# Chain stages one whole step apart, weight pieces among the first nine loads, two filler products a unit in the first pass

## The chip, the cores and the metric

The kernel runs on one core of a Trainium2 chip. The metric is device time in microseconds (us), the median of several executions. A profile's own span, from first to last instruction, is 1.7 to 1.9 us shorter than the time of the same run. In the profile, PE is the tensor engine (PEld its weight loads), DVE the vector engine, ACT the scalar engine, POOL the GpSimd engine, SP the engine that issues the output transfers.

## The reference, cut to what matters

Four batches of 12480 rows of 128 numbers, 32 inducing rows, then a feed-forward with a gelu on every output row:

```python
def mab(q, kv):
    s = scale * (q @ kv.transpose(0, 2, 1))
    s = s - s.max(-1, keepdims=True)
    a = np.exp(s)
    a /= a.sum(-1, keepdims=True) + 1e-09
    return a @ kv
h = mab(I, x)            # 32 rows per batch: needs the whole batch
out = mab(x, h)          # every row of x against the 32 rows of h
# then, with x = out as 49920 rows:
h = x @ w_in                                   # 128 -> 2048
g = 0.5 * h * (1.0 + erf(h * inv_sqrt2))
return g @ w_out                               # 2048 -> 128
```

For these inputs the gelu can be expanded and moved in front of the second attention, onto the 32 rows of h. So the kernel makes two passes over the rows with a small dense computation, the "chain", between them for each batch, and checks on the device that the expansion was good enough (`check_gelu`).

## The kernel before

A batch is 7 units: six of 2048 rows and a tail of 192. The kernel issues work in steps. Step s transposes unit s, scores unit s-1, and adds unit s-2 into the sums of pass one; 21 steps later it runs pass two (`b_...`) for a unit. Steps 0 to 20 are pass one alone, 21 to 28 are both passes, and from about 29 it is pass two alone. In this kernel's timelines a product that waits for DVE holds up all products behind it: in chain 0 qp waited 2.35 us for gl, and PE ran nothing from 43.81 to 46.16 us. In the chain, pt is the projection of the 32 rows of h by w_in, sl and gl are the two steps of the expanded gelu on it, and qp is the product of gl with w_out; hs, slope and offs are small sums and factors for sl and gl.

```python
def a_load(u):                       # fp32 -> fp16, from POOL's queue
    xh = sb.tile([128, 16, 128], FP16, tag="xh", bufs=9)
    nc.gpsimd.dma_start(out=xh[: u.p, : u.nc, :], in_=src)

def a_score(bt, u):
    s1 = ps.tile([128, 16, M], FP32, tag="sc", bufs=2)
    ...                              # 16 products of 128x32 on PE
    nc.scalar.activation(out=e1t..., in_=s1..., func=AF.Exp, scale=SCALE)
    ...
    nc.gpsimd.tensor_tensor(out=acc, in0=acc, in1=e1t[: u.p, : u.nc, :], op=ALU.add)

def precompute(bt):                  # the chain; one stage per next()
    ...                              # stage 0: hun_sb (ACT), r1s (DVE, from acc)
    yield
    ...                              # h_ps (PE)
    yield
    ...                              # rr1, range checks, hT (DVE)
    yield
    ...                              # pt_ps = w_in_h.T @ hT: 16 products (PE)
    yield
    pt = pre.tile([128, NBLK, M], FP32, tag="pt")
    nc.scalar.activation(out=pt, in_=pt_ps, func=AF.Copy)
    nc.gpsimd.tensor_tensor(out=zsq, in0=pt, in1=pt, op=ALU.mult)
    nc.vector.tensor_reduce(out=hs, in_=pt, axis=AX.X, op=ALU.add)
    yield
    ...                              # slope, offs: 128x16 (DVE)
    nc.vector.tensor_tensor(out=sl, in0=pt, in1=slope..., op=ALU.mult)     # 128x512, SBUF
    yield
    nc.vector.tensor_tensor(out=gl, in0=sl, in1=offs..., op=ALU.subtract)  # 128x512, SBUF
    yield
    ...                              # qp_ps: 16 products of gl with w_out_h (PE)
    yield
    ...                              # qp (ACT)
    yield
    ...                              # q_ps (PE), q (DVE)
    yield
    check_gelu(bt, zsq, hs)          # seven small DVE operations

# in at_step(s); pump() runs one stage of the oldest chain, twice a step
if a0: a_transpose(bat(a0), a0, 0)
if a1: a_score(bat(a1), a1)
pump()
...
if a0: a_transpose(bat(a0), a0, 1)
if b0: b_score(bat(b0), b0)
pump()
...
if a2:
    a_gather(bat(a2), a2)
    if a2.tail:
        chains.append(precompute(bat(a2)))
    load_next()
    if weight_loads and s % 2:       # steps 3, 5, 7, 9
        dst, src = weight_loads.pop(0)
        nc.gpsimd.dma_start(out=dst, in_=src)
```

## Time and profile before

| | before |
|---|---|
| time, median of the first three runs | 165.76 us |
| span of the profiled run | 163.8 us |
| bytes of loads as landed (x as fp16, and weights) | 13.83 MB |
| bytes of output | 25.58 MB |
| step 21's score of pass two starts | 75.33 us |
| the same of steps 28 and 35 | 100.81, 120.45 us |

I use those three starts throughout as marks: the end of pass one alone, of both passes, and of the next batch.

The page's 40 slices of the span, kernel before: granted PE clock in tenths (the share of its full clock rate that PE was given), and the mean busy share of the 16 DMA engines in tenths. A slice is 4.1 us.

```profile
PEclk9999999655775599965999959755555555555555
DMA  3999999999999599895067367569678799999990
```

DMA is full for 12 slices from the second on, and then for longer only in the last ones. Between them it has gaps, and in pass one the clock falls to half three times (at 29.8, 46.8 and 70.7 us). The grant changes at 29.75, 43.41, 46.82, 57.06, 70.71 and 77.54 us in this trace, and these times lie multiples of 3.413 us apart.

The PE timeline of the kernel before, chain 0. Columns: start, length, engine and line, operation, how many, and in brackets the idle time before it and what ended it.

```profile
34.11 0.37 PE L276 MATMUL pt_ps<-hT,w_in_h 128*128 128x32 f16 x8 [0.33 <-DVE hT L271]
38.08 0.39 PE L276 MATMUL pt_ps<-hT,w_in_h 128*128 128x32 f16 x8 [3.60 <-DMA w_in_h<-in_moe_w_in_dram]
...
46.16 0.30 PE L328 MATMUL qp_ps<-w_out_h,gl 128*32 128x128 f16 x8 [2.35 <-DVE gl L318]
48.67 0.41 PE L328 MATMUL qp_ps<-w_out_h,gl 128*32 128x128 f16 x8 [2.21 <-DMA w_out_h<-in_moe_w_out_dram]
```

The chain's products stop PE four times here, for w_in, for gl, for w_out, and (0.33 us) for hT. Taking all PE idle times above 0.5 us from 5 us to step 21's score in the timeline together, 6.44 us were waits for rows of x and 15.15 us were other waits, all but 0.62 us of them in the chains.

POOL's timeline shows what that does to the loads: the load at 49.82 us was issued 4.27 us late because its turn came after a transpose on the halted PE.

```profile
44.41 1.14 POOL L177 TENSOR_TENSOR acc<-acc,e1t 128x512 f32<-128x512 f32 x1 [0.45 <-ACT e1t L170]
49.82 0.57 POOL L83 DMA_DIRECT2D xh<-in_x_dram  x1 [4.27 <-PE tr L150]
```

Busy times by stretch, kernel before, steps 21 to 28 and 28 to 35. Columns: stretch, length, then busy us (and count) of PE, PEld, DVE, ACT, POOL, then mean granted clock, DMA share and GB/s.

```profile
75.33:100.81 25.48, 23.21 (x394) 14.54 (x394) 21.96 (x51) 16.50 (x30) 13.21 (x14) 0.89 0.51 205
100.81:120.45 19.64, 14.16 (x205) 8.62 (x205) 16.53 (x45) 10.72 (x22) 12.77 (x16) 0.60 0.69 280
```

### The profile page before, as it was taken

The page shows a single profiled execution, that of the slowest core. Times are in us where ns is not written, and L with a number is a line of the kernel's source. Part 1 is how long each engine was busy: PE and PEld are TensorE (multiplying, and loading weights), DVE is VectorE, ACT ScalarE, POOL GpSimd, SP SyncE. Part 2 cuts the span into 40 slices and gives each one's busy share as a digit, 9 for nine tenths or more (in the row PEclk, how much of TensorE's full clock was granted, in tenths as well). Part 3 has the DMA queues.
Part 4 walks back from the last instruction along what each step waited for, and adds up shares of the span by engine and source line. Part 5 has one row for each costly group of instructions (what it writes and reads, how often), then busy time and mean ns, then how long its engine had stood idle before and what let it go on. Part 6 is the DMA issues. An engine that isn't in the chain of part 4 may idle for free. (4 is left out here: it accounts for less than half of the span.)

```text
span 163.8 us, 4550 instructions
## 1 busy us (share of the span) xinstructions
PE 111.2 (68%) x1859; PEld 77.4 (47%) x1859; DVE 91.6 (56%) x229; ACT 79.5 (49%) x136; POOL 93.1 (57%) x117
## 2 busy tenths in 40 slices
PE   0388587737617988369999598698458986678300
PEld 0366576626515877258666344363224543334100
DVE  2123132321822644926897988878989865467600
ACT  3057465431701465614867545648154774567300
POOL 7615866651815264942456825678374996589600
PEclk9999999655775599965999959755555555555555
DMA  3999999999999599895067367569678799999990
GB/s 39 213 214 215 213 212 207 194 209 202 214 204 208 95 204 175 146 156 99 32 288 320 136 256 318 222 288 392 250 316 320 306 416 420 392 375 418 420 380 18
DMA packets 10249, 39.74 MB, mean 243 GB/s; under 512 B 3024, under 2 KB 3824, under 8 KB 7152
## 3 DMA queue, kind: packets, MB, share of 16 engines
q0 software_dynamic: 6272, 13.83, 46.0%
q1 hardware_dynamic: 3952, 25.58, 38.3%
q8 instruction: 15, 0.25, 0.6%
q14 instruction: 10, 0.08, 0.2%
HBM read 27.67 MB, written 25.56 MB: 325 GB/s over the span
## 5 line engine op out<-in xcount | busy, mean ns | idle before, releaser
L150 PE MATMUL tr<-identity_h,xh 128*128 128x128 f16 x392 | 37.4, 252 | 7.6 <-DMA xh<-in_x_dram 7.1
L401 ACT ACTIVATE o<-at 128x512 f32<-128x512 f32 (+1 forms) x43 | 25.4, 591 | 20.9 <-PE at L440 13.4
L150 PEld LDWEIGHTS <-xh 128*128 128x128 f16 x392 | 28.4, 113 | 14.8 <-DMA xh<-in_x_dram 8.7
L177 POOL TENSOR_TENSOR acc<-acc,e1t 128x512 f32<-128x512 f32 (+1 forms) x24 | 24.3, 1012 | 19.3 <-ACT e1t L170 19.2
L83 POOL DMA_DIRECT2D xh<-in_x_dram x28 | 15.7, 565 | 14.1 <-PE tr L150 5.8
L402 POOL TENSOR_TENSOR o<-o,rr_1999 128x512 f32<-128x512 f32 x12 | 12.5, 1048 | 5.7 <-issue 2.0
L402 POOL TENSOR_TENSOR o<-o,rr_2618 128x512 f32<-128x512 f32 x12 | 12.3, 1047 | 3.6 <-ACT o L401 3.5
L402 POOL TENSOR_TENSOR o<-o,rr_2348 128x512 f32<-128x512 f32 x12 | 12.3, 1047 | 3.7 <-ACT o L401 3.3
L155 DVE COPY xT_459<-tr 128x1024 f16<-128x1024 f16 (+1 forms) x7 | 4.4, 628 | 17.0 <-PE tr L150 17.0
L404 DVE TENSOR_TENSOR o<-at,rr_1431 128x512 f32<-128x512 f32 (+1 forms) x19 | 12.0, 666 | 1.5 <-PE at L413 0.8
L155 DVE COPY xT_120<-tr 128x1024 f16<-128x1024 f16 (+1 forms) x7 | 4.4, 630 | 13.4 <-PE tr L150 13.4
L404 DVE TENSOR_TENSOR o<-at,rr_2618 128x512 f32<-128x512 f32 (+1 forms) x13 | 8.5, 670 | 4.6 <-DMA out_dram<-o 3.0
L404 DVE TENSOR_TENSOR o<-at,rr_2348 128x512 f32<-128x512 f32 (+1 forms) x13 | 8.5, 668 | 3.7 <-DMA out_dram<-o 1.8
L187 PEld LDWEIGHTS <-e1t 128*32 128x32 f16 x392 | 7.5, 109 | 5.6 <-issue 4.5
L404 DVE TENSOR_TENSOR o<-at,rr_1999 128x512 f32<-128x512 f32 (+1 forms) x13 | 8.6, 669 | 2.5 <-PE at L440 1.4
L157 ACT ACTIVATE xT_120<-tr 128x1024 f16<-128x1024 f16 x6 | 6.1, 1019 | 6.8 <-PE tr L150 6.8
L328 PE MATMUL qp_ps<-w_out_h,gl 128*32 128x128 f16 x64 | 2.3, 274 | 9.8 <-DVE gl L318 7.5
L402 POOL TENSOR_TENSOR o<-o,rr_1431 128x512 f32<-128x512 f32 (+1 forms) x7 | 6.6, 949 | 3.0 <-issue 1.6
L155 DVE COPY xT_895<-tr 128x1024 f16<-128x1024 f16 (+1 forms) x7 | 4.4, 628 | 6.5 <-PE tr L150 6.5
L175 POOL CAST acc<-e1t 128x512 f32<-128x512 f16 x4 | 2.4, 612 | 8.4 <-ACT e1t L170 8.4
L157 ACT ACTIVATE xT_1339<-tr 128x1024 f16<-128x1024 f16 x6 | 6.2, 1031 | 0.8 <-PE tr L150 0.8
L328 PEld LDWEIGHTS <-gl 128*32 128x32 f16 x64 | 1.2, 113 | 11.3 <-DVE gl L318 8.9
(352 smaller groups left out, 245.0 us busy)
## 6 DMA issues: line engine op xcount, KB each, us to landing
out_dram<-o SPq DMA_DIRECT2D x24, 1024.0 KB, 5.1
xh<-in_x_dram POOLq DMA_DIRECT2D x24, 512.0 KB, 11.1
w_in_h<-in_moe_w_in_dram POOLq DMA_DIRECT2D x2, 256.0 KB, 14.4
w_out_h<-in_moe_w_out_dram POOLq DMA_DIRECT2D x2, 256.0 KB, 14.2
out_dram<-o SPq DMA_DIRECT2D x4, 96.0 KB, 4.9
xh<-in_x_dram POOLq DMA_DIRECT2D x4, 48.0 KB, 8.3
ind_s<-in_inducing_dram SPq DMA_DIRECT2D x1, 16.0 KB, 1.6
```

Of the source, the lines that this page charges most:

```text
L83: nc.gpsimd.dma_start(out=xh[: u.p, : u.nc, :], in_=src)
L150: nc.tensor.transpose(tr[:, c - c0, : u.p], xh[: u.p, c, :], identity_h[: u.p, : u.p])
L155: nc.vector.tensor_copy(out=dst, in_=tr[:, : c1 - c0, : u.p])
L157: nc.scalar.activation(out=dst, in_=tr[:, : c1 - c0, : u.p], func=AF.Copy)
L175: nc.gpsimd.tensor_copy(out=acc, in_=e1t)
L177: nc.gpsimd.tensor_tensor(out=acc, in0=acc, in1=e1t[: u.p, : u.nc, :], op=ALU.add)
L187: nc.tensor.matmul(bt.hun[32 * j : 32 * j + 32, :], e1t[: u.p, j * u.nci + ci, :], xh[: u.p, j * u.nci + ci, :], start=(u.idx == 0 and ci ...
L328: nc.tensor.matmul(qp_ps[32 * j : 32 * j + 32, :], gl[:, blk, :], w_out_h[:, blk, :], start=(blk < 4), stop=(blk >= NBLK - 4),)
L401: nc.scalar.activation(out=dst, in_=at, func=AF.Copy)
L402: nc.gpsimd.tensor_tensor(out=dst, in0=dst, in1=by, op=ALU.mult)
L404: nc.vector.tensor_tensor(out=dst, in0=at, in1=by, op=ALU.mult)
```

## The change

Its intent: a product of the chain should find its operand ready; the weights should be there before chain 0 needs them; and two full-array products a unit, whose results are overwritten, should keep PE's clock up while pass one runs alone. Cut to its core:

```diff
-    def a_score(bt, u):
+    def a_score(bt, u, n_warm):
         s1 = ps.tile([128, 16, M], FP32, tag="sc", bufs=2)
+        for _ in range(n_warm):
+            nc.tensor.matmul(s1.rearrange("p (k c) m -> p k (c m)", k=4), identity_h,
+                x_tiles[(u.b, u.idx)][:, 0:4, :], start=True, stop=True)
@@ precompute
-        hun_sb = pre.tile([128, C], FP32, tag="hun_sb")     # and r1s: bufs=2
+        hun_sb = pre.tile([128, C], FP32, tag="hun_sb", bufs=2)
         ...                                    # r1s
         yield
+        yield
         ...                                    # h_ps
-        in_range(rr1, 1.0 / R_HIGH, 1.0 / R1_LOW, bt.b, 0)
         ...                                    # hT
-
+        in_range(rr1, 1.0 / R_HIGH, 1.0 / R1_LOW, bt.b, 0)
+        yield
         yield
         pt_ps = ps.tile([128, NBLK, M], FP32, tag="misc")
         ...                                    # pt | slope, sl | gl: unchanged
+        yield
         yield
         qp_ps = ps.tile([128, 128], FP32, tag="misc")
         ...                                    # qp
+        yield
         yield
         q_ps = ps.tile([128, 128], FP32, tag="misc")
@@ at_step
-            a_score(bat(a1), a1)
+            a_score(bat(a1), a1, 0 if b0 or a1.tail else 2)
...
                 chains.append(precompute(bat(a2)))
+                next(chains[-1])
             load_next()
-            if weight_loads and s % 2:
-                dst, src = weight_loads.pop(0)
-                nc.gpsimd.dma_start(out=dst, in_=src)
@@ before step 0
-    for _ in range(7):
+    for _ in range(3):
         load_next()
+    for dst, src in weight_loads:
+        nc.gpsimd.dma_start(out=dst, in_=src)
+        load_next()
```

More of the change, by code (lines that the diff above doesn't have):

```diff
@@ L157, in a_transpose @@
             nc.scalar.activation(out=dst, in_=tr[:, : c1 - c0, : u.p], func=AF.Copy)
-    def a_score(bt, u):
+    def a_score(bt, u, n_warm):
         s1 = ps.tile([128, 16, M], FP32, tag="sc", bufs=2)
+        for _ in range(n_warm):
+            nc.tensor.matmul(
+                s1.rearrange("p (k c) m -> p k (c m)", k=4),
+                identity_h,
+                x_tiles[(u.b, u.idx)][:, 0:4, :],
+                start=True,
+                stop=True,
+            )
         for c in range(u.nc):
@@ L255, in precompute @@
     def precompute(bt):
-        hun_sb = pre.tile([128, C], FP32, tag="hun_sb")
+        hun_sb = pre.tile([128, C], FP32, tag="hun_sb", bufs=2)
         nc.scalar.activation(out=hun_sb, in_=bt.hun, func=AF.Copy)
-        r1s = pre.tile([128, M], FP32, tag="r1s")
+        r1s = pre.tile([128, M], FP32, tag="r1s", bufs=2)
         nc.vector.tensor_reduce(
```

## The prediction

> **What bounds the kernel now**, from the busy times by stretch and the timelines:
>
> (1) First pass alone (steps 0 to 20), to 73.4 us, where unit 21's transposes start. Loads land 212 GB/s (5 to 50 us); loads with weights are 13.83 MB (DMA queues), 65 us, so unit 21 could land near 57 us. It starts 16 us later because the in-order PE stalls in the chain: 0.86 (r1s), 0.33 (hT), 3.60 (w_in), 2.35 (gl), 2.21 (w_out), 0.91 us (qp) in chain 0, and 4.6 us in chain 1. After each long stall the granted clock is 0.5 (30 to 44, 47 to 57, 71 to 78 us): eight transposes take 0.82 us instead of 0.45, and a unit costs PE 2.7 us instead of 1.65, more than the 2.47 us in which one lands. Late gathers free buffers late: POOL waits 4.27 us before the load at 49.8 us; DMA falls to 0.42 at 54 to 57 us.
>
> (2) Both passes (steps 21 to 28), 75 to 103 us: DVE busy 4.0 to 4.9 of each 5 us, some 3.3 us a step.
>
> (3) Second pass alone: batch 1 takes 103 to 124 us where its writes need 15 (6.4 MB at 417 GB/s): stalls of 1.08, 2.81 and 2.10 us on the last chain. Batches 2 and 3 (124 to 155 us) are bound by the writes.
>
> **What changes.** The same chain work (about 7.8 us of DVE a chain) spreads over seven steps instead of five, and PE products find operands half a step or more old. Weights (1.05 MB, 5 us) land among units 5 to 8, delay those by up to 5 us, and steal nothing later. POOL issues 13 loads before its first accumulation; the ninth already waited for the first landing, so accumulation 0 comes near 17 us instead of 11.4, absorbed later. Added: 36 fillers on PE, estimated at 0.21 us each at full clock (0.43 at half): 1.65 + 0.43 = 2.1 us a unit stays under 2.47. Removed: 15 us of PE stalls in the first pass, 3 to 6 in batch 1.
>
> [...] This trace's grants change at multiples of 3.413 us[...].
>
> **Critical path.** First pass becomes bound by loads: unit 21 starts at 57 to 62 us (-11 to -16). Steps 21 to 28 then share DMA between the last loads (12.6 us) and their writes (15), so they take 27 to 30 us. Batch 1: 17 to 18 us (-3 to -4). The rest is unchanged: 31 us bound by writes, 9 of ending.
>
> 58 + 29 + 18 + 31 + 9 + 2 (time over span) = 147; 2 more for clock dips. **149 us, 143 to 156**. Faster by over 2%: 0.93, within 2%: 0.05, slower: 0.02.
>
> **Signs.** PE idle at pt, qp and q products nearly gone; clock 1.0 through most of the first 60 us; DMA above 0.95 to about 75 us; unit 21's transposes at 57 to 62 us; batch 1 under 19 us.
>
> **What would make it wrong.** Fillers that don't hold the clock: a unit then costs PE 2.7 + 0.86 us, unit 21 starts near 68 us, the time is near 157. Late POOL accumulations that stall the exps. Steps 21 to 28 at half clock[...]. Loads and writes together slower than 420 GB/s.

That the fillers would hold the clock was the estimate; a_nofill below measures it (mean granted clock from 6.6 us to step 21: 0.91 with them, 0.83 without). Their cost is measured in the changed kernel's PE timeline: after two of them the next product starts 0.43 us later at full clock and 0.85 us at half, so 0.215 and 0.43 us each. The four groups of products that a step of pass one gives PE, two of transposes, a score and a gather, take 1.74 us from start to start at full clock (19.92 to 21.66 us, kernel before) and 2.79 at half (38.96 to 41.75), near the 1.65 and 2.7 of the prediction.

## The result, and the profile after

| | before | after |
|---|---|---|
| time, median | 165.55 us (4 runs) | 160.49 us (4 runs) |
| ratio | 1 | 0.970 (95% interval 0.965 to 0.975) |
| step 21's score of pass two | 75.33 us | 70.79 us |
| steps 21 to 28 | 25.48 us | 25.27 us |
| steps 28 to 35 | 19.64 us | 19.40 us |
| from step 35's score to the end of the span | 43.4 us | 43.2 us |

A ratio here is the mean time of one kernel's fast runs over that of the other's of the same rounds, so it is not quite the ratio of the medians. All four runs of the changed kernel were fast. It is faster by 3%, not by 10%. That it would be faster by over 2% held; the predicted range, 143 to 156 us, misses the time by 4.5 us. All of the gain comes before step 21; the rest only moves forward.

The page's slices after (4.0 us each):

```profile
PEclk9999977959997899987999999655555555555555
DMA  2999999999999999893177449459977999998990
```

DMA is full for 15 slices now, nearly so for two more, and the mean granted clock from 6.6 us to step 21's score rose from 0.79 to 0.91 (busy times by stretch). Then DMA has the same hole as before.

The PE timeline after, same columns:

```profile
21.59 0.62 PE L150 MATMUL tr<-identity_h,xh 128*128 128x128 f16 x8 [2.81 <-DMA xh<-in_x_dram]
...
31.10 0.62 PE L150 MATMUL tr<-identity_h,xh 128*128 128x128 f16 x8 [2.06 <-DMA xh<-in_x_dram]
...
44.55 0.77 PE L171 MATMUL s_856<-indT,xT_473 128*128 128x32 f16 x16
48.28 0.41 PE L339 MATMUL qp_ps<-w_out_h,gl 128*32 128x128 f16 x16 [2.95 <-DVE gl L328]
...
49.37 0.93 PE L150 MATMUL tr<-identity_h,xh 128*128 128x128 f16 x8
...
68.80 0.41 PE L339 MATMUL qp_ps<-w_out_h,gl 128*32 128x128 f16 x16 [3.03 <-DVE gl L328]
```

Two things are seen. First, PE waits for rows longer at the start (2.81 us, 2.06 us), because the weights land in front of them: idle times above 0.5 us for data are 9.14 us, against 6.44. Step 10 starts at 37.1 us, and before at 31.5. Second, the wait for gl at qp is still there in both chains, 2.95 and 3.03 us, where it was 2.35 and 2.38. After the first the clock is at half again, 0.50 from 49.5 to 52.9 us (eight transposes in 0.93 us instead of 0.61). The other waits in the chains went: non-data waits are 6.77 us, against 15.15.

The stages before qp on DVE, after:

```profile
43.16 0.69 DVE L299 TENSOR_REDUCE hs<-pt 128x16 f32<-128x512 f32 x1 [2.53 <-ACT pt L295]
...
44.37 0.17 DVE L302 TENSOR_SCALAR slope<-hs 128x16 f32<-128x16 f32 x1
...
44.56 1.97 DVE L320 TENSOR_TENSOR sl<-pt,slope 128x512 f32<-128x512 f32 x1
46.57 1.66 DVE L328 TENSOR_TENSOR gl<-sl,offs 128x512 f16<-128x512 f32 x1
48.15 0.25 DVE L155 COPY xT_473<-tr 128x192 f16<-128x192 f16 x1
```

And POOL in the same window:

```profile
43.21 1.04 POOL L297 TENSOR_TENSOR zsq<-pt 128x512 f32<-128x512 f32 x1 [0.49 <-ACT pt L295]
44.19 0.59 POOL L83 DMA_DIRECT2D xh<-in_x_dram  x1
44.81 1.17 POOL L186 TENSOR_TENSOR acc<-acc,e1t 128x512 f32<-128x512 f32 x1
45.91 0.57 POOL L83 DMA_DIRECT2D xh<-in_x_dram  x1
46.50 1.17 POOL L186 TENSOR_TENSOR acc<-acc,e1t 128x512 f32<-128x512 f32 x1
```

The operation sl is listed with 1.97 us, gl with 1.66 us; at their best the same operations take 0.68 and 0.67 us in the two traces. Their ends stand in a fixed relation to POOL: the accumulation at 44.81 ends at 45.98 and sl at 46.53, 0.55 us later; the accumulation at 46.50 ends at 47.67 and gl at 48.23, 0.56 us later. That looks like operations that waited for POOL and then ran. In the list they are simply long: no idle time is shown. In chain 2 of the same run no POOL operation lies beside sl (90.61 us), and it takes 0.69 us. Which operation goes first isn't settled: sl's recorded start, 44.56 us, is 0.25 us before that of the accumulation, 44.81 us, and sl still ended after it; the profile's own notes call spans on POOL rough. The 128x16 operation slope, too, took 1.65 us beside an accumulation in chain 1 and 0.17 us in chain 0; in a_psum its longest was 0.92 us. No run isolates it.

Busy times by stretch, after:

```profile
70.79:96.06 25.27, 22.35 (x394) 14.23 (x394) 20.86 (x50) 16.95 (x29) 13.67 (x15) 0.95 0.52 197
96.06:115.46 19.40, 13.83 (x205) 8.21 (x204) 16.51 (x46) 10.63 (x22) 12.80 (x15) 0.62 0.77 311
```

### The profile page after: what moved, and what is told of

The parts are those of the page before. It is cut to its first block, busy times and chain, and to the rows that moved or that the text cites. A ratio compares the mean times of both kernels' runs of the same rounds, so it can differ in the third digit from the quotient of the medians.

```text
span 158.7 us, 4622 instructions
## 1 busy us (share of the span) xinstructions
PE 113.9 (72%) x1895; PEld 76.4 (48%) x1895; DVE 92.2 (58%) x229; ACT 80.3 (51%) x136; POOL 94.1 (59%) x117
## 3 DMA queue, kind: packets, MB, share of 16 engines
q1 hardware_dynamic: 3952, 25.58, 39.6%
HBM read 27.67 MB, written 25.56 MB: 335 GB/s over the span
## 5 line engine op out<-in xcount | busy, mean ns | idle before, releaser
L150 PE MATMUL tr<-identity_h,xh 128*128 128x128 f16 x392 | 34.3, 239 | 9.6 <-DMA xh<-in_x_dram 9.1
L413 ACT ACTIVATE o<-at 128x512 f32<-128x512 f32 (+1 forms) x43 | 25.4, 591 | 22.6 <-PE at L452 12.4
L150 PEld LDWEIGHTS <-xh 128*128 128x128 f16 x392 | 26.1, 107 | 16.5 <-DMA xh<-in_x_dram 10.3
L186 POOL TENSOR_TENSOR acc<-acc,e1t 128x512 f32<-128x512 f32 (+1 forms) x24 | 24.5, 1019 | 13.0 <-ACT e1t L179 12.8
L414 POOL TENSOR_TENSOR o<-o,rr_2025 128x512 f32<-128x512 f32 x12 | 12.9, 1086 | 6.0 <-DVE rr_2025 L405 2.6
L414 POOL TENSOR_TENSOR o<-o,rr_2654 128x512 f32<-128x512 f32 x12 | 12.4, 1048 | 3.8 <-ACT o L413 3.7
L414 POOL TENSOR_TENSOR o<-o,rr_2372 128x512 f32<-128x512 f32 x12 | 12.5, 1048 | 3.4 <-ACT o L413 1.6
L196 PEld LDWEIGHTS <-e1t 128*32 128x32 f16 x392 | 6.7, 100 | 4.9 <-issue 3.2
L299 DVE TENSOR_REDUCE hs<-pt 128x16 f32<-128x512 f32 x4 | 2.7, 686 | 7.0 <-ACT pt L295 7.0
```

What stands on the lines that cost most here:

```text
L150: nc.tensor.transpose(tr[:, c - c0, : u.p], xh[: u.p, c, :], identity_h[: u.p, : u.p])
L196: nc.tensor.matmul(bt.hun[32 * j : 32 * j + 32, :], e1t[: u.p, j * u.nci + ci, :], xh[: u.p, j * u.nci + ci, :], start=(u.idx == 0 and ci ...
L413: nc.scalar.activation(out=dst, in_=at, func=AF.Copy)
L414: nc.gpsimd.tensor_tensor(out=dst, in0=dst, in1=by, op=ALU.mult)
```

## The experiments

The theory after the comparison: the qp wait is what eats the gain of pass one; it stays because sl and gl are held up (1.97 and 1.66 us, at best 0.68 and 0.67) beside POOL's accumulations, which read SBUF as they do; early weights pay at the start what they save later; fillers are worth little; and steps 21 to 35 don't move because DVE paces them. All experiments start from the changed kernel ("a_..."), unless said otherwise, and all gave right results. Times are medians of four runs each, in which slow runs are named; ratios are to the kernel before on the same chip.

| run | time us | ratio to before (95%) | step 21 | 21 to 28 | 28 to 35 |
|---|---|---|---|---|---|
| changed kernel | 160.49 | 0.970 (0.965-0.975) | 70.79 | 25.27 | 19.40 |
| a_nofill | 159.53 | 0.967 (0.958-0.976) | 70.95 | 25.22 | 19.38 |
| a_oldweights | 161.30 | 0.978 (0.969-0.987) | 71.89 | 25.09 | 19.40 |
| a_oldchain | 166.50 | 1.013 (1.003-1.023) | 75.81 | 23.93 | 19.63 |
| only_chain | 160.97 | 0.977 (0.971-0.982) | 71.27 | 25.12 | 19.40 |
| a_gap | 154.88 | 0.941 (0.931-0.952) | 64.95 | 25.54 | 18.33 |
| a_gap_nofill | 152.22 | 0.922 (0.917-0.926) | 63.33 | 25.30 | 17.65 |
| a_psum | 152.95 | 0.923 (0.919-0.927) | 65.43 | 24.03 | 19.16 |
| a_psum_hs | 153.80 | 0.930 (0.927-0.933) | 65.54 | 24.03 | 19.16 |
| a_gap_late | 150.78 | 0.902 (0.898-0.907) | 62.43 | 25.56 | 18.34 |
| a_nocheck | 154.88 | 0.936 (0.928-0.943) | 69.82 | 24.32 | 16.76 |
| best_psum_late | 153.01 | 0.923 (0.915-0.932) | 61.67 | 24.84 | 19.16 |
| best_psum_gap_late | 147.45 | 0.894 (0.889-0.898) | 61.26 | 22.43 | 18.09 |

One run of a_oldchain, a_nocheck and best_psum_late and two of a_gap_late were slow (over 1.5% above their fastest), and so was one run of the kernel before; the profile of a_gap_late is of a slow run. The ratios leave them out, the medians don't. Stretches and waits are of one profiled run each.

### Which of the three parts: a_nofill, a_oldweights, a_oldchain, only_chain

Fillers out:

```diff
-            a_score(bat(a1), a1, 0 if b0 or a1.tail else 2)
+            a_score(bat(a1), a1, 0)
```

> The changed kernel without the 36 filler products. Theory A (fillers earn their cost by holding the clock): with half-clock stretches back in steps 10 to 20, the b-score of step 21 comes 2 to 4 us later than the changed kernel's 70.8 us, and the time is 162 to 164 us. Rival B (once the chain stalls are shorter, the load stream alone keeps PE warm, and the fillers are 0.43 us a unit on an in-order PE that sets the pace from step 10): step 21 comes 2 to 4 us earlier and the time is 156 to 158.5 us.

Neither theory: 159.53 us, a ratio that isn't separated from the changed kernel's, and step 21 at 70.95 us. The clock is a little lower without fillers (mean 0.83 from 6.6 us to step 21, against 0.91), and PE has less to do (47.0 us busy against 50.8); step 21 comes at the same time. The fillers raise the clock. It buys nothing here.

Weights back at steps 3, 5, 7 and 9:

```diff
-    for _ in range(3):
+    for _ in range(7):
         load_next()
-    for dst, src in weight_loads:
-        nc.gpsimd.dma_start(out=dst, in_=src)
-        load_next()
@@ at_step
             load_next()
+            if weight_loads and s % 2:
+                dst, src = weight_loads.pop(0)
+                nc.gpsimd.dma_start(out=dst, in_=src)
```

> The changed kernel with the weight pieces issued at steps 3, 5, 7 and 9 again. Theory A (weights in front cost up to 5.6 us of waiting for data in steps 0 to 10, as much as the two weight waits they remove): step 10 starts at 31 to 32 us instead of 37.1, then PE waits 2 to 6 us for weights at the products of pt and qp; the time is within 1.5 us of 160.5. Rival B (early weights are a plain gain of the 5.8 us of weight waits): the time is 164 to 166 us.

Theory A: 161.30 us, within 1.5 us. The PE timeline has the two waits for weights back:

```profile
37.83 0.39 PE L286 MATMUL pt_ps<-hT,w_in_h 128*128 128x32 f16 x8 [2.08 <-DMA w_in_h<-in_moe_w_in_dram]
...
48.40 0.40 PE L339 MATMUL qp_ps<-w_out_h,gl 128*32 128x128 f16 x8 [3.90 <-DMA w_out_h<-in_moe_w_out_dram]
```

Waits for data fall from 9.14 to 6.01 us and the others rise from 6.77 to 9.80. Early weights move about as much waiting as they remove.

Chain stages half a step apart again:

```diff
@@ precompute, in all four places: before h_ps, pt_ps, qp_ps and q_ps
         yield
-        yield
@@ the range check of rr1 again before hT, hun_sb and r1s in one buffer each
@@ at_step
                 chains.append(precompute(bat(a2)))
-                next(chains[-1])
```

> The changed kernel with the chain's stages half a step apart again. Theory A (spacing helps, but left a 3 us stall a chain in place): the chain stalls of 4.6 us a chain are back in the first pass against 3.0 and 3.8, and the time is 161.5 to 164 us; step 21 to 35 lengths stay at about 25.3 and 19.5 us. Rival B (spacing is the main source of the gain): 164 to 166 us, with steps 21 to 35 longer as well.

166.50 us, above both ranges: the spacing is all of the gain, but not by the waits I had counted. PE's idle time from 37.1 us to step 21 is only 1.3 us longer than in the changed kernel. The rest is that PE is busy longer with the same products (30.5 us to 75.8, against 26.8 us to 70.8; mean clock there 0.87 against 0.94); what keeps the clock lower there no run isolates. Steps 21 to 35 aren't longer (43.6 us against 44.7), which rival B wanted.

Spacing alone, in the kernel before:

```diff
@@ the changed kernel with the edits of a_nofill and a_oldweights together
-            a_score(bat(a1), a1, 0 if b0 or a1.tail else 2)
+            a_score(bat(a1), a1, 0)
...
+            if weight_loads and s % 2:
+                dst, src = weight_loads.pop(0)
+                nc.gpsimd.dma_start(out=dst, in_=src)
```

> The kernel before with the spaced chain stages alone: weights at steps 3, 5, 7, 9, no fillers. Theory A (the spacing is the whole gain; the early weights and the fillers together are worth nothing): 159.5 to 162 us, weight waits of 2 and 4 us at pt and qp as in a_oldweights. Rival B (the three parts need each other): 163 us or more.

160.97 us, theory A: the spacing by itself does what the whole change does, within the intervals. Fillers and early weights together, without it (a_oldchain), give nothing.

### The wait at qp: a_gap, a_psum, a_psum_hs

One more whole step between gl and qp:

```diff
         nc.vector.tensor_tensor(out=gl, ...)
         yield
         yield
+        yield
+        yield
         qp_ps = ps.tile([128, 128], FP32, tag="misc")
```

> The changed kernel with one more whole step between the gl stage and the qp products. Theory A (in the first pass the PE waits 2.95 and 3.03 us at qp because gl is issued only half a step of PE time ahead, and the clock falls after it): both waits go to under 0.5 us, the clock stays at 1.0 from 40 us to 70 us, step 21 comes 5 to 8 us earlier, and the time is 153 to 156 us. Rival B (what is won before step 21 is lost again because steps 21 to 28 then share DMA with the last loads): step 21 earlier by as much, but the time is 157.5 to 160 us.

Theory A: 154.88 us, step 21 5.8 us earlier, and steps 21 to 28 not longer (25.54 us). qp waits for nothing any more. But the same delay of DVE still stops PE, at another product:

```profile
47.61 0.26 PE L171 MATMUL s<-indT,xT 128*96 128x32 f16 x2 [2.23 <-DVE xT L155]
...
48.26 0.41 PE L341 MATMUL qp_ps<-w_out_h,gl 128*32 128x128 f16 x16
```

In a_gap sl and gl still take 1.97 and 1.66 us in chain 0, so a transposed unit behind them is copied late and a score waits 2.23 us for it. The extra step hides most of the delay; it doesn't take it away.

sl and gl computed in place in PSUM, where the projection already lies:

```diff
-        sl = pre.tile([128, NBLK, M], FP32, tag="sl")
         nc.vector.tensor_tensor(
-            out=sl, in0=pt,
+            out=pt_ps, in0=pt_ps,
             in1=slope.unsqueeze(2).broadcast_to([128, NBLK, M]), op=ALU.mult)
         ...
-            out=gl, in0=sl,
+            out=gl, in0=pt_ps,
```

> The changed kernel with the products sl and gl computed from the PSUM copy of the projection, in place, so that neither reads two large tiles from SBUF. Theory A (sl took 1.97 us and gl 1.66 us in chain 0, against 0.69 us at best, because POOL's accumulation, which also reads SBUF, ran at the same time): both take under 0.8 us in all four chains, the wait at the first qp falls from 2.95 us to about 0.7, the second (slope 1.65 us in place of 0.17) falls by less, step 21 comes 2.5 to 4.5 us earlier, time 156 to 158.5 us. Rival B (the lengths come from something else, such as the recorded start of the operation): sl and gl stay above 1.2 us where POOL is busy, time 160 to 161 us.

152.95 us, better than theory A's range, without any change in the order of instructions. The same two operations on DVE in a_psum:

```profile
44.71 0.70 DVE L319 TENSOR_TENSOR pt_ps<-pt_ps,slope 128x512 f32<-128x512 f32 x1
45.44 0.69 DVE L327 TENSOR_TENSOR gl<-pt_ps,offs 128x512 f16<-128x512 f32 x1
46.05 0.25 DVE L155 COPY xT<-tr 128x192 f16<-128x192 f16 x1
```

with POOL accumulating beside them as before:

```profile
44.95 1.17 POOL L186 TENSOR_TENSOR acc<-acc,e1t 128x512 f32<-128x512 f32 x1
46.05 0.57 POOL L83 DMA_DIRECT2D xh<-in_x_dram  x1
46.64 1.17 POOL L186 TENSOR_TENSOR acc<-acc,e1t 128x512 f32<-128x512 f32 x1
```

and the qp wait that remains:

```profile
46.19 0.41 PE L338 MATMUL qp_ps<-w_out_h,gl 128*32 128x128 f16 x16 [0.72 <-DVE gl L327]
```

sl and gl take 0.70 and 0.69 us at most in all four chains, against 1.97 and 1.66 us. (The edit also moves sl's output to PSUM; gl writes to SBUF as before and is freed as well, so the operand read is what counts for gl.) POOL's accumulation is as long as before (1.17 us) and overlaps them freely. Waits other than for data fall from 6.77 to 2.14 us, step 21 comes 5.4 us earlier, steps 21 to 28 are 1.2 us shorter. So in this kernel what made sl take 1.97 us and gl 1.66 beside POOL's accumulations goes when the large operand is read from PSUM. I had not allowed for it in the prediction.

hs from PSUM too:

```diff
-        nc.vector.tensor_reduce(out=hs, in_=pt, axis=AX.X, op=ALU.add)
+        nc.vector.tensor_reduce(out=hs, in_=pt_ps, axis=AX.X, op=ALU.add)
```

> As a_psum, and hs is reduced from PSUM too, so that DVE doesn't wait 2.53 us for ACT's copy of the projection. Theory A (the qp wait is the sum of DVE's wait for ACT and of POOL holding DVE up): the two qp waits of 2.95 and 3.03 us go to under 0.5 us without a longer chain, step 21 comes at 64 to 67 us, time 154 to 157 us, as a_gap. Rival B (DVE has only moved its idle time): no more than 0.5 us better than a_psum.

153.80 us, no better than a_psum, as rival B has it. But the edit didn't take the wait away, so the run tests neither theory. In a_psum_hs DVE still waits 2.53 us before hs, for ACT's copy:

```profile
43.13 0.69 DVE L299 TENSOR_REDUCE hs<-pt_ps 128x16 f32<-128x512 f32 x1 [2.53 <-ACT pt L295]
```

The products of pt_ps end at 41.09 us by the PE timeline and ACT's copy of them at 43.09 us; hs starts after the copy, though it no longer reads it. What the wait for ACT is worth stays open. It isn't what made the qp wait 2.95 us: in a_psum it is still 2.53 us long, and the qp wait is 0.72 us.

### Fillers and weights once the wait is gone: a_gap_nofill, a_gap_late

a_gap with the edit of a_nofill:

```diff
-            a_score(bat(a1), a1, 0 if b0 or a1.tail else 2)
+            a_score(bat(a1), a1, 0)
```

> a_gap without the 36 filler products. Theory A (fillers are worth nothing: the clock falls in the same places with and without them, after PE waits): time within 1.5 us of a_gap's 154.9. Rival B (with the long waits gone, only the fillers hold the clock): 157 us or more, with half clock between 40 and 65 us.

Better than both theories: 152.22 us, 2.7 us below a_gap, with ratios whose intervals don't touch (0.917-0.926, 0.931-0.952), though from two calls. The clock is lower without fillers (mean 0.88 against 0.94 to step 21) and step 21 still comes 1.6 us earlier. The 36 products of 0.215 us (after two of them the next product starts 0.43 us later at full clock, 0.85 us at half) are 7.7 us of PE's time; that they cost more here because PE paces more of pass one fits, but isn't shown: PE's waits for data are 10.87 us without them against 8.92. And 0.9 us of the gain lies in steps 21 to 35, where neither kernel has fillers; that part isn't explained.

a_gap with weight pieces at steps 2, 3, 5 and 6 (and seven loads before step 0, as in a_oldweights):

```diff
+            if weight_loads and s in (2, 3, 5, 6):
+                dst, src = weight_loads.pop(0)
+                nc.gpsimd.dma_start(out=dst, in_=src)
```

> a_gap with the weight pieces issued at steps 2, 3, 5 and 6 instead of before step 0. Theory A (the weights in front hold steps 5 to 9 up by 5 us of DMA, later they land while PE is behind the loads): PE waits for data in steps 0 to 9 fall from 8.9 us to 3 to 5, no product waits over 0.7 us for a weight, step 21's b-score comes at 59.5 to 62 us and the time is 149.5 to 152.5 us. Rival B (step 21 earlier, but steps 21 to 28 then wait for the last loads, which share DMA with the writes): 153 to 155 us.

The fast runs took 148.77 and 149.75 us, on both sides of theory A's lower edge; the profile, of a slow run of 151.82 us, has step 21 at 62.43 us, no wait over 0.5 us for a weight, and 6.83 us of waiting for data in place of 8.92. Steps 21 to 28 didn't stretch. In this kernel the right time for the weights is after the units that PE is waiting for, and before the chain wants them.

### What paces steps 21 to 35: a_nocheck

```diff
-        check_gelu(bt, zsq, hs)
+    # at the start: gelu_sums set to constants that pass
```

> The changed kernel without the check of the gelu expansion (about 2.0 us of DVE a chain; its sums are set to constants that pass; the output stays right). Theory A (steps 21 to 35 are paced by DVE, which was busy 38 of 45 us there, so spacing the chain can't shorten them and dropping work can): steps 21 to 28 take 23 to 24.3 us instead of 25.3, steps 28 to 35 16.5 to 17.8 instead of 19.4, time 155.5 to 158 us. Rival B (they are paced by latency between engines or by the writes): under 0.7 us in each, 159.5 to 160.5 us.

Theory A, and a little more in time than I expected (154.88 us). The stretches:

```profile
69.82:94.14 24.32, 22.03 (x395) 14.33 (x394) 19.28 (x43) 16.73 (x29) 13.69 (x15) 0.94 0.57 208
94.14:110.90 16.76, 13.29 (x206) 7.67 (x205) 14.28 (x38) 10.46 (x22) 12.76 (x15) 0.67 0.89 360
```

Taking 1.6 us of busy DVE out of steps 21 to 28 shortened them by 0.95 us (25.27 to 24.32); taking 2.2 us out of steps 28 to 35 shortened them by 2.6 us (19.40 to 16.76), near the 15 us that this batch's output needs, an estimate from a quarter of the 25.58 MB of output and the prediction's 417 GB/s (the four fullest slices of the page of the kernel before have 416 to 420 GB/s). So DVE's work counts here. That spacing which leaves this work in place can't shorten these steps, as theory A also has it, is not so: the extra step of a_gap alone took steps 28 to 35 from 19.40 to 18.33 us, and below it takes steps 21 to 28 from 24.84 to 22.43 us. In the changed kernel the check of one chain and the first stage of the next even fall into one step, and PE waited 3.08 us at step 30 for r1s. DVE's timeline there, changed kernel:

```profile
99.04 0.67 DVE L223 TENSOR_REDUCE ssq<-zsq 128x16 f32<-128x512 f32 x1
99.63 1.05 DVE L225 SCALAR_TENSOR_TENSOR left<-hs 128x16 f32<-128x16 f32 x1
...
101.40 0.68 DVE L416 TENSOR_TENSOR o<-at,rr_2025 128x512 f32<-128x512 f32 x1
102.00 1.00 DVE L268 TENSOR_REDUCE r1s<-acc 128x32 f32<-128x512 f32 x1
```

Without the check that wait is 0.75 us; with the extra step of a_gap it is under 0.5 us, because the order of the two stages changes. Dropping the check thus removes both work and a wait, and how much of the 2.6 us is which isn't separated.

### Putting it together: best_psum_late, best_psum_gap_late

a_psum with weights at steps 2, 3, 5, 6 (and seven loads before step 0) and no fillers:

```diff
@@ a_psum
-            a_score(bat(a1), a1, 0 if b0 or a1.tail else 2)
+            a_score(bat(a1), a1, 0)
...
+            if weight_loads and s in (2, 3, 5, 6):
+                dst, src = weight_loads.pop(0)
+                nc.gpsimd.dma_start(out=dst, in_=src)
```

> The changed kernel with sl and gl computed in PSUM (a_psum), weight pieces at steps 2, 3, 5, 6 and no fillers. Theory A (the three add: 7.5 us from PSUM, 3 to 4 from late weights, 1 to 2.5 from no fillers): step 21's b-score at 57 to 61 us, time 146 to 149.5 us. Rival B (steps 21 to 28 stretch to 27 us or more, because the last loads share DMA with the writes): 150 to 152 us.

A miss: 153.01 us (fast runs 151.08 to 153.13), no better than a_psum, though step 21 came at 61.67 us and not 65.43. Part of the gain in pass one is lost after it: steps 21 to 35 take 44.0 us against 43.2, and there is a 3.08 us wait for r1s (2.73 in a_psum). The runs also scatter more than the others'. Where the rest went I can't say: no profile of a 153 us run exists.

The same with the extra step before qp:

```diff
@@ best_psum_late
         yield
         yield
+        yield
+        yield
         qp_ps = ps.tile([128, 128], FP32, tag="misc")
```

> best_psum_late with the extra step before qp (a_gap). Theory A (with gl in time the extra step has nothing left to remove in the first pass, but moves the r1s stage away from the previous chain's check, which cost 3.08 us at step 30): 0.5 to 2 us faster than best_psum_late. Rival B (no effect): within 0.5 us of it.

147.45 us, far more than the 0.5 to 2 us of theory A, and its four runs lie within 0.3 us. It beats both kernels: 0.894 of before (0.889 to 0.898), and its median is 8% below the changed kernel's. It was run at another time.

```profile
PEclk9999999995599999999999995555555555555555
DMA  2999999999999999999978775999949989799970
```

```profile
61.26:83.69 22.43, 20.88 (x395) 13.58 (x394) 19.94 (x48) 16.73 (x30) 14.06 (x17) 1.00 0.92 290
83.69:101.78 18.09, 15.50 (x205) 9.33 (x204) 16.69 (x47) 11.19 (x22) 13.33 (x16) 0.62 0.84 338
```

DMA is full for 19 slices of 3.6 us and nearly full through steps 21 to 28, which take 22.43 us, 2.8 less than in the changed kernel, while DMA carries 290 GB/s instead of 197. Waits for data, 12.4 us of idle PE before step 21, are nearly all that is left there: the first pass is bound by the loads, as I had forecast, at 61.3 us. The wait for r1s is gone. The extra step changed nothing before step 21 (61.26 us against 61.67) and took 3.5 us out of steps 21 to 35, with the same work on DVE.

## Why the prediction was wrong

- **The first pass, 57 to 62 us: wrong, and the step that failed.** The prediction said "PE products find operands half a step or more old", removed "15 us of PE stalls in the first pass", and put step 21 at 57 to 62 us. Its transposes started at 69.4 us. Non-data waits fell from 15.15 to 6.77 us, so 8.4 us went and not 15, while waits for data grew by 2.7 us. The term that was mis-sized most is the qp wait, 2.95 + 3.03 us where nothing was to be left: I costed sl and gl by their work in the chain as a whole, and took half a step to be enough. Beside POOL's accumulations they take up to 1.97 and 1.66 us, against 0.68 and 0.67 at best, and both lie together right before qp. The trace of before had it: gl took 1.52 us there in chain 0 and 0.67 at best. a_psum, where the same two take 0.70 and 0.69 us with one operand in PSUM, shows the cause, and a_psum and a_gap the size: step 21 comes 5.4 and 5.8 us earlier. The best kernel's step 21 is 9.5 us earlier; late weights with no fillers give 3.8 of that (a_psum to best_psum_late), so the other two parts of the change were mis-sized too.
- **Early weights: half right.** The delay of "up to 5 us" came (step 10 5.6 us later), and the weight waits of 5.8 us went. I counted the removed waits as gain along with a first pass bound by loads, which holds only when nothing else stops PE. Alone the move is worth nothing that these runs separate.
- **Fillers: cost right, worth wrong.** They take 0.215 us each and raise the clock (mean 0.91 against 0.83 in a_nofill), but a higher clock brought no time: without them the time is the same, and 2.7 us better in a_gap (1.6 us of that before step 21). The prediction's warning, unit 21 near 68 us and a time near 157 if the fillers fail, comes near the measured 69.4 and 160.5 us by luck: the fillers did raise the clock.
- **POOL's first accumulation near 17 us: right** (17.26 us), and it did no harm that the profile shows.
- **Steps 21 to 28, 27 to 30 us: wrong the other way.** They took 25.3 us, as before. Soon after step 21 began all loads had landed (DMA share 0.51 from 70 to 75 us, 0.02 from 74 to 76). Even where step 21 came at 61.3 us, in the best kernel, sharing DMA didn't lengthen them.
- **Batch 1, 17 to 18 us: wrong.** Between the same marks it is 19.40 us, against 19.64. DVE was busy 16.5 us in both. PE's waits mostly moved: before 1.08, 2.81 and 2.10 us, after 3.08, 1.41 and 0.89 (the last of each after step 35). The spacing chosen put one chain's check and the next chain's r1s into one step; with one more step (a_gap) batch 1 took 18.33 us, and 17.65 in a_gap_nofill, a gain of 2.0 us where 3 to 4 was forecast.
- **The rest, 42 us: 45.0.** I counted the last two batches from the end of batch 1's outputs, 124 us, not from step 35's score. By the same mark the kernel before has 45.1 us, so the 3.0 is a wrong boundary.

The sum closes: 147 us predicted (without the 2 us for clock dips), + 12.8 for step 21 (70.8 against 58), - 3.7 for steps 21 to 28 (25.3 against 29), + 1.4 for batch 1, + 3.0 for the rest is 160.5 us, the measured time. Nearly all of the error is the first term (1.4 us of it is that the 58 was forecast for unit 21's transposes and 70.8 is its score's mark). With the stall alone taken away the change gives 152.95 us (a_psum), or 154.88 with one step more (a_gap): inside the range. The best kernel's 147.45 us is no proof of the forecast, since it also puts the weights late and has no fillers.

## What to carry to other kernels

When stages of a chain are moved apart, look at each operation's longest time in the trace and not its mean, and ask who runs beside it: here sl and gl, reading SBUF alone, took 1.97 and 1.66 us of busy time beside POOL's accumulations, with no idle time shown, and 0.70 and 0.69 us once one operand was read from PSUM. Where DVE was busy about 85% of a stretch, taking work from it helped (a_nocheck, steps 28 to 35 from 19.40 to 16.76 us), but so did one more step of spacing that kept two chains' DVE stages apart (a_gap, 18.33 us): check which stages of neighbouring chains fall into one step. The transfers put "early" delayed what the kernel was waiting for at that moment (step 10 started at 37.1 us, not 31.5), and the products that only raise the clock brought no time here, at a mean clock of 0.91 against 0.83, and cost 2.7 us once the long waits were gone.
